# First products of the first two pairs as 256-column matmuls, under a new list of steps

## The chip, the cores and the metric

The kernel runs on one core of a Trainium2 chip. The metric is the device time of one execution in microseconds (us). The engines that matter here are TensorE (PE, with its weight loads shown as PEld), VectorE (DVE), ScalarE (ACT), GpSimd (POOL) and SyncE (SP).

## The reference

A linear attention with a decaying state feeds a two-layer network:

```python
# r, k, v: (4, 8, 768, 48); w, u: (8, 48); w_in: (384, 2048); w_out: (2048, 384)
for t in range(S):
    cur = einsum('bhd,bhe->bhde', u * k[t], v[t])
    y[t] = einsum('bhd,bhde->bhe', r[t], state + cur)
    state = w * state + einsum('bhd,bhe->bhde', k[t], v[t])
x = y.transpose(0, 2, 1, 3).reshape(B * S, H * D)      # 3072 x 384
h = x @ w_in
out = maximum(0.01 * h, h) @ w_out                     # 3072 x 384
```

## The kernel before, in words

The 3072 tokens are cut into 24 **stages** of 128 tokens, numbered 0 to 23, six to a batch. Inside a batch a stage hands its state to the next one. Two stages that follow each other form a **pair**, 0 to 11; the network works on pairs.

Nothing is scheduled at run time. One string, `ORDER` (lines 31 to 72), lists about 880 **steps** by short names, and the loop at line 801 records them in that order. Each engine then plays its own steps strictly in the listed order, and waits on semaphores only where a step reads or overwrites what a step of another engine made (`Sched`, lines 79 to 159). So the list decides two things: which step stands behind which on its engine, and what a waiting step holds up behind it. A step's name is a letter, then the stage or pair and a part, and behind `@` the PSUM bank or banks (0 to 7) that it opens. A bank can be opened again only when all readers of what was in it are done.

The letters, with the engine that plays them:

- `k`, `r`, `v` with a stage: loads of its inputs, issued by POOL; `i` with a number: a quarter of `w_in`; `w` with a number: a quarter of `w_out`, both issued by POOL. Stage 0's r and k are `p2` and `p3` and go by SP and ACT.
- `p` with a number: one-time steps. Among them `p21` (PE, spreads the row w), `p22` to `p24` (ACT, its log and two tables), `p25` and `p26` (the table of u), `p27` to `p30` (ACT, the decay over a stage, `wl`), `p16` and others (DVE, constants). `q`: DVE clears the padding of a buffer.
- `F1.512.12`: a fill; PE multiplies a matrix of ones with 512 columns (or 256, or 128) of ones, and nobody reads it (line 374).
- `P`: DVE scales r and k by the tables into `qk`. `T`, `C`: PE turns one half of `qk` (4 matmuls, line 413), ACT copies it out. From stage 8 on, `X` does the turn by a DMA transpose from SP (stages 6 and 7 and those before are turned on PE).
- `D`: DVE multiplies the turned halves (stages 0 to 5). `E`, `f`, `R`: DVE makes the diagonal's sums for the later stages. `L`: POOL spreads them into a tile.
- `A`: PE's scores (8 matmuls, line 473). `M`: DVE masks them into `at`; for some halves ACT copies (`m`) and DVE masks in place (`N`).
- `K`: PE's keys times values, for stages 0 to 5 with the diagonal's sums, for stages 1 and 2 with the carried state added (lines 527 to 536). `V`: DVE scales v by those sums. `B`, `W`: DVE makes the next state.
- `Y`: PE's outputs of a stage (lines 601 and 605). `O`: ACT copies them as `xT`.
- First product: `G` (line 634) makes four of the 16 blocks of the hidden layer for one stage, `J` (line 656) two blocks for both stages of a pair. `g` (line 644) and `j` (line 665): ACT's leaky ReLU of one such bank into `gT`.
- Second product of a pair, `w_out`: a Strassen-like scheme of seven products. `t`: DVE's sums of `w_out`'s blocks. `b`: DVE's sums of `gT`'s blocks (line 726). `Z0.0` to `Z0.6`: the seven products on PE (8 matmuls each, line 757). `z0.0` to `z0.6` (and `z11.7`): ACT or DVE takes the sums out. `o`: SP stores a stage, or half of it.

In the kernel before, pairs 0 and 1 (stages 0 to 3) go by `G`, 16 of them, and pairs 2 to 11 by `J`, 80 of them. The two differ in the columns of a matmul and in what they wait for:

```python
def up_one(n, grp):                       # G
    for f in range(4):
        for s in range(NSL):              # 3 slices of 128 of x
            PE.matmul(ps[i][:, 128 * f:128 * f + 128], w_in_sb[:, s, 128 * fb:128 * fb + 128], xT[ix][:, s, t], ...)
    add("pe", emit, R=[("xT", ix, half), ("win", grp)], W=[key])
def up_two(m, j):                         # J
    for f in range(2):
        for s in range(NSL):
            PE.matmul(ps[i][:, 256 * f:256 * f + 256], w_in_sb[:, s, 128 * fb:128 * fb + 128], xT[ix][:, s, :], ...)
    add("pe", emit, R=[("xT", ix, 0), ("xT", ix, 1), ("win", j // 2)], W=[key])
```

Of the kernel before, what the change touches and what calls it, by code (L numbers as in the profile page):

```python
# [46 lines left out]
z2.0 z0.6 J4.1@0 P15 X11 E13 J4.0@1 B9 j4.1 R10 J3.5@2 j3.4 f12 X13 L10 f13 J4.7@3 j3.5 P14 J3.7@0 j4.0 z1.5 R11
X15 Z1.6 W9 r19 b2.3 J4.4@4 o1 R12 r22 J4.5@5 X14 j4.4 j4.7 L12 A10@12 Z2.1@4 j3.7 M10 o0 k22 j4.5 K10@3 Z2.2
z1.6 B10 o3 L11 J4.6@5 R13 o2 A12@01 j4.6 L13 A11@23 M12 J4.3@7 k16 J4.2@5 M11 Z3.0@0 r16 j4.2 Z2.3@1 z2.2 W10
z2.1 b2.2 j4.3 A13@23 E15 Y10@5 f15 Y11@7 R15 Z2.4 O11 M13 O10 L15 Z2.5 z3.0 J5.6@7 k19 E14 b3.0 J5.2@5 k17 b3.1  # L50
J5.3@2 j5.2 z2.4 v13 Z3.1@3 b4.0 z2.5 J5.1@5 v14 b3.3 K12@4 Z2.6 j5.1 k23 B12 j5.3 Z3.2 z2.3 f14 k18 o4 b3.2
J5.4@5 R14 v15 A15@12 j5.4 b4.1 J5.7@4 j5.6 v20 M15 Z3.3@5 z3.2 z2.6 r17 j5.7 J5.5@7 z3.3 z3.1 K13@6 L14 Z3.4
B13 J5.0@1 z3.4 r18 b4.2 A14@45 W13 Z4.0@2 v18 M14 Z3.5 z4.0 k21 j5.5 K14@6 Z3.6 z3.5 v19 B14 Z4.1@7 P19 z3.6
j5.0 r21 W14 K15@0 P17 Y13@3 Y14@1 E18 r20 X17 b5.2 Y12@4 O14 Y15@5 f18 Z4.2 b4.3 O15 o6 O12 B15 Z4.3@1 o5 z4.1
z4.2 P18 J7.2@0 O13 E16 R18 J7.4@6 E19 z4.3 J6.5@5 E17 P16 Z4.4 j6.5 b5.0 X16 J6.6@1 f16 R16 J6.0@3 X19 b5.1 L16
J6.1@4 j6.0 E22 J6.7@5 f17 j6.1 f19 X18 z4.4 Z4.5 j7.2 R19 j6.7 J6.4@3 R17 v22 P21 o7 J6.2@0 z4.5 L17 X21 Z4.6
j6.2 L18 J7.5@7 z4.6 j7.4 J7.1@0 j6.4 L19 A16@45 j7.5 A17@23 M16 j7.1 v23 J7.7@6 Z5.0@7 k20 j7.7 M17 J6.3@0 j6.6
v21 z5.0 A19@45 j6.3 A18@12 r23 K16@6 M18 J7.6@3 Z5.1@0 j7.6 W15 K19@1 M19 J7.0@2 z5.1 Z5.2 j7.0 b6.0 Z6.0@3 B16
Z5.3@2 b5.3 z6.0 z5.2 K18@4 W16 J7.3@5 B18 Z5.4 z5.3 B19 Y16@6 b6.2 Y17@4 E21 Y18@2 E20 Y19@1 f21 z5.4 Z5.5 O19
b6.1 O18 Z6.1@1 R21 O16 P20 O17 J9.1@2 L21 j7.3 W19 X20 Z5.6 j9.1 b7.2 J8.3@6 J9.2@2 P23 z5.5 J8.0@4 X23 f22 P22  # L60
J8.2@5 f20 b7.0 Z6.2 o9 j8.2 o8 R22 J8.4@0 j9.2 X22 b6.3 j8.0 J8.7@5 R20 z6.2 j8.3 Z6.3@2 E23 L20 b7.1 j8.7
J9.0@4 z6.1 f23 j8.4 Z6.4 R23 b7.3 J9.3@0 L22 J8.5@6 z6.4 j9.3 z6.3 K20@5 Z6.5 j8.5 L23 B20 j9.0 Z6.6 z6.5 z5.6
o12 J9.6@2 z6.6 o10 J9.7@0 o11 j9.6 o13 A22@34 j9.7 A20@12 M22 A21@56 J8.6@7 J9.4@0 W20 M21 Z7.0@3 j9.4 J8.1@4
z7.0 M20 Z7.1@0 j8.1 Z7.2 j8.6 b8.0 Y21@1 Y20@2 O21 A23@45 O20 Z8.0@1 M23 J10.6@2 z8.0 b8.1 J10.3@6 K21@7 J9.5@4
B21 J10.7@5 j9.5 J10.0@7 j10.3 b9.0 z7.2 Z7.3@4 z7.1 W21 K22@6 Z7.4 B22 Z7.5 z7.4 b9.1 Z8.1@6 z7.3 Z7.6 z7.5 W22
b9.3 J10.1@4 z7.6 j10.7 b8.2 o15 Z9.0@0 j10.0 b8.3 J10.5@3 b9.2 Z8.2 j10.5 z9.0 Y22@5 j10.6 Y23@7 J10.2@3 O23
O22 J10.4@2 j10.1 J11.0@7 z8.2 j10.2 J11.3@5 z8.1 j10.4 J11.2@4 b10.0 Z8.3@3 j11.2 b10.1 Z8.4 j11.0 z8.3 j11.3
Z8.5 b10.2 Z10.0@7 z8.4 b10.3 Z9.1@2 z10.0 Z8.6 J11.5@3 z8.6 o17 J11.1@1 o14 J11.6@4 j11.1 Z9.2 j11.5 j11.6
Z10.1@5 z9.1 z9.2 J11.7@1 Z9.3@3 j11.7 J11.4@4 z10.1 Z9.4 j11.4 Z11.0@1 b11.0 Z9.5 b11.2 Z10.2 z8.5 z9.4 o16
b11.1 Z10.3@4 z10.2 z9.3 Z11.1@6 z9.5 o18 Z9.6 Z10.4 z9.6 z11.0 o19 z11.1 Z10.5 z10.4 Z11.2@0 Z11.3 z11.2 b11.3  # L70
Z10.6 z11.3 z10.5 Z11.4 z11.7 z10.6 z10.3 o23.1 Z11.5 o21 z11.4 o23.0 Z11.6@1 z11.5 o20 o22.1 z11.6 o22.0
"""


# [786 lines left out]
```

## Time and profile before

| | |
|---|---|
| median of 3 runs | 168.54 us (168.5 to 168.78) |
| the profiled execution | 168.21 us |
| its span, first to last instruction | 166.4 us |
| busy, PE / DVE / ACT / POOL | 156.9 / 129.0 / 88.5 / 89.7 us |
| matmuls on PE | 2362 |
| DMA | 19.69 MB in 100092 packets |

The span is what the trace shows; 1.8 us of the execution lie around it. Busy time of PE counts a matmul from its start to its modelled end, so overlapping ones are not counted twice, and a matmul that waits inside the pipeline counts as busy. Idle time of an engine costs only where another waits for it.

### The profile page before, as it was taken

What the parts mean: (1) busy time and instruction counts of PE and PEld (TensorE: products, weight loads), DVE (VectorE), ACT (ScalarE), POOL (GpSimd) and SP (SyncE); (2) the same over time, 40 slices, a digit from 0 to 9 for tenths busy, and PEclk for the clock granted to TensorE, in tenths of its full rate; (3) what the DMA queues carried; (4) which work ended last, traced back from release to release, by engine and by line L of the source; (5) the groups of instructions that cost most, each with busy time, mean ns of one, the idle gap of its engine ahead of it and who ended that gap; (6) DMA issues with size and microseconds to landing.
All of it is one profiled execution on the core that took longest, in us unless ns stands there. A gap on an engine that the chain in (4) does not pass through costs nothing.

```text
span 166.4 us, 5494 instructions
## 1 busy us (share of the span) xinstructions
PE 156.9 (94%) x2362; PEld 138.9 (83%) x2362; DVE 129.0 (78%) x261; ACT 88.5 (53%) x195; POOL 89.7 (54%) x101
## 2 busy tenths in 40 slices
...
GB/s 98 117 117 143 146 191 168 162 204 183 141 137 143 119 134 154 192 213 69 149 98 128 195 138 154 67 4 98 190 149 44 0 4 47 6 2 96 47 96 189
DMA packets 100092, 19.69 MB, mean 118 GB/s; under 512 B 93154, under 2 KB 100068, under 8 KB 100068
## 3 DMA queue, kind: packets, MB, share of 16 engines
...
q1 hardware_dynamic: 22514, 9.12, 26.8%
...
## 4 chain that ended last, share of the span: by engine, by line
PE 77%; DVE 11%; issue 3%; DMA 3%; ACT 2%; POOL 2%; DVEq 0%; POOLq 0%
PE ps_all L757 30%; PE ps_all L656 28%; PE ps_all L601 5%; PE ps_all L634 4%; PE ps_all L473 4%; DMA rk_sb<-in_r_dram 3%; DVE gs L726 2%; PE ps_all L413 2%; POOL rk_sb L274 2%; PE ps_all L531 2%; DVE ku L434 2%; DVE s_tok L444 1%; DVE at L497 1%; DVE qk L391 1%; ACT tp L424 1%
## 5 line engine op out<-in xcount | busy, mean ns | idle before, releaser
L665 ACT ACTIVATE gT<-ps_all 128x512 bf16<-128x512 f32 x80 | 44.8, 604 | 31.9 <-PE ps_all L656 28.6
L656 PE MATMUL ps_all<-xT,w_in_sb 128*128 128x256 bf16 x480 | 58.9, 273 | 0.1
L656 PEld LDWEIGHTS ps_all<-xT,w_in_sb 128*128 128x128 bf16 x480 | 45.5, 98 | 5.7 <-DVE out_sb L778 0.3
L459 POOL TENSOR_SCALAR_AFFINE_SELECT at<-s_tok 128x1024 bf16<-128x1024 f32 x18 | 22.3, 1254 | 31.7 <-DVE s_tok L444 31.7
L726 DVE TENSOR_TENSOR gs<-gT 128x1024 bf16<-128x1024 bf16 x24 | 17.8, 745 | 15.6 <-ACT gT L665 8.4
L757 PE MATMUL ps_all<-tw,gs 128*128 128x192 bf16 x288 | 28.9, 246 | 0.0
L497 DVE CAST_PREDICATED at<-mask,ps_all 128x1024 bf16<-128x1024 uint16 x18 | 21.7, 1219 | 6.6 <-PE ps_all L473 6.2
L757 PEld LDWEIGHTS ps_all<-tw,gs 128*128 128x128 bf16 x288 | 24.0, 98 | 0.7
L274 POOL DMA_DIRECT2D v_sb<-in_v_dram x24 | 22.6, 960 | 0.0
L274 POOL DMA_DIRECT2D rk_sb<-in_r_dram x23 | 21.8, 956 | 0.3 <-issue 0.3
L274 POOL DMA_DIRECT2D rk_sb<-in_k_dram x23 | 21.3, 937 | 0.0
L757 PE MATMUL ps_all<-w_out_sb,gT 128*128 128x192 bf16 x192 | 19.5, 246 | 0.0
L768 ACT ACTIVATE snap<-ps_all 128x192 f32<-128x192 f32 x36 | 11.3, 341 | 11.9 <-PE ps_all L757 11.8
L757 PEld LDWEIGHTS ps_all<-w_out_sb,gT 128*128 128x128 bf16 x192 | 16.1, 98 | 0.6
L619 ACT ACTIVATE xT<-ps_all 128x384 bf16<-128x384 f32 x24 | 11.0, 494 | 10.5 <-PE ps_all L601 8.7
L778 DVE TENSOR_TENSOR out_sb<-ps_all,snap 128x192 f32<-128x192 f32 x37 | 12.4, 351 | 2.9 <-PE ps_all L757 2.7
L391 DVE TENSOR_TENSOR qk<-rk_sb,tab 128x768 bf16<-128x768 bf16 x23 | 12.6, 550 | 2.2 <-DMA rk_sb<-in_r_dram 1.2
L634 PE MATMUL ps_all<-xT,w_in_sb 128*128 128x128 bf16 x192 | 12.4, 219 | 0.4 <-issue 0.2
L634 PEld LDWEIGHTS ps_all<-xT,w_in_sb 128*128 128x128 bf16 x192 | 11.0, 98 | 1.0 <-issue 0.4
L601 PE MATMUL ps_all<-at,v_sb 128*32 128x128 bf16 x384 | 10.7, 220 | 0.9 <-issue 0.9
L644 ACT ACTIVATE gT<-ps_all 128x512 bf16<-128x512 f32 x16 | 8.8, 603 | 4.6 <-PE ps_all L634 4.6
L424 ACT ACTIVATE tp<-ps_all 128x512 bf16<-128x512 f32 x16 | 8.8, 596 | 4.4 <-PE ps_all L413 4.3
...
## 6 DMA issues: line engine op xcount, KB each, us to landing
...
tp<-qk SPq DMA_TRANSPOSE x16, 4.2
```

Of the source, the lines that this page charges most:

```text
L274: add("pool", lambda: G.dma_start(dst, src), W=[key], dma=f"{which}{n}")
L391: add("dve", lambda: V.tensor_tensor(qk[iq][:, :, 0:D], both, by, ALU.mult), R=[("r", n % NRK), ("k", n % NRK), "qtab", "ktab", ("qk0", iq ...
L459: add("pool", lambda: G.affine_select(out=at[ia][:, :, :, :].rearrange("p two m i -> p (two m) i"), in_=s_tok[i2][:, :].unsqueeze(2).to_br ...
L497: add("dve", lambda: V.copy_predicated(dst, mask[:, :].bitcast(mybir.dt.uint16).unsqueeze(1).to_broadcast([128, H, 128]), raw), R=keys + [ ...
L601: last = PE.matmul(ps_y[32 * q:32 * q + 32, 128 * s:128 * s + 128], a, m, start=first_mm and (s == 0 or whole), stop=last_mm and whole)
L634: last = PE.matmul(ps[i][:, 128 * f:128 * f + 128], w_in_sb[:, s, 128 * fb:128 * fb + 128], xT[ix][:, s, t], start=s == 0, stop=s == NSL - 1)
L656: last = PE.matmul(ps[i][:, 256 * f:256 * f + 256], w_in_sb[:, s, 128 * fb:128 * fb + 128], xT[ix][:, s, :], start=s == 0, stop=s == NSL - 1)
L665: add("act", lambda: A.activation(gT[ig][:, 2 * j:2 * j + 2, :].rearrange("p f t -> p (f t)"), ps[i][:, :], AF.Prelu, alpha=0.01), R=[key] ...
L726: add(eng, lambda: on.tensor_tensor(x[i][:, :, :], a, b, op), R=keys, W=[("gs", m % 2, i)])
L757: done = PE.matmul(ps[i][:, 0:NH], lhs[:, s, :], rhs[:, s, :], start=bool(opens) and s == 0, stop=s == HF - 1, skip_group_check=not (opens ...
L768: add("act", lambda: A.activation(snap[i2][j][:, :], ps[i][:, 0:NH], AF.Copy), R=[key], W=[("snap", i2, j)])
L778: add("dve", lambda: V.tensor_tensor(out_sb[io][:, cols], ps[i][:, 0:NH], snap[i2][j][:, :], ALU.add), R=[key, ("snap", i2, j), *after], W ...
```

## The change

Two things are edited, both in `ORDER`; no function changes. Pairs 0 and 1 now go by `J` and `j` as the others do: 16 `G` and 16 `g` leave the list, `J0.0` to `J0.7`, `J1.0` to `J1.7` and their `j` come in. And the whole list is in another order, with other PSUM banks, and with 23 fills in place of 11 (7,296 columns in place of 3,840). All other steps are the same set. The start, up to the first second product, of the old list and the new:

```diff
-p1 p0 p9 p19 q4 p18 p2 r2 q1 p3 q3 p15 p4 p11 p8 q2 p10 p5 p21@0 k2 q0 p14 p13 p12 p17 p6 p16 k1 p7 F1.512.12@1
-p22 r1 p20 p23 k5 p24 P0.0 r5 P0.1 T0.0@7 q5 F1.512.6@6 p31 v0 C0.0 F1.256.8@5 P2 T0.1@6 r3 p25@7 C0.1 T2.1@0 k3
-T2.0@1 P1 C2.1 D0 T1.1@2 v1 p32 T1.0@0 C1.1 P5 F1.512.1@3 i1 C1.0 F1.256.11@4 A0@23 C2.0 v2 D1 A1@45 M0.1 p27
-p28 A2@01 k6 F1.512.3@6 T5.1@3 F1.256.7@6 C5.1 P3 F1.256.9@6 r6 T5.0@6 m1.1 M0.0 T3.1@3 p29 k4 M2 K0@5 p30
-T3.0@2 C3.1 v3 C5.0 F1.256.4@3 B0 F1.256.13@0 C3.0 V0 r4 K1@3 D2 A3@56 B1 r7 F1.256.3@0 Y0@1 M3.0 K2@2 k7 M1.0
-O0 p26 A5@01 N1.1 i0 G0.1@5 D3 V2 i3 P6 g0.1 Y2@4 v4 V1 T6.0@7 M5.0 O2 T6.1@5 r9 Y1@3 C6.0 D5 B2 C6.1 K3@4 k9
-G2.1@0 P4 O1 m5.1 M3.1 T4.0@7 r8 T4.1@5 C4.0 V3 G1.1@2 P7 C4.1 i2 Y3@3 N5.1 g1.1 v7 E7 T7.1@1 B3 O3 A4@56 D4 v5
-T7.0@7 f7 C7.0 E6 G2.0@2 v6 f6 C7.1 R6 G0.0@7 g2.1 k8 M4 G3.1@1 L6 G1.0@0 g3.1 W3 G3.0@3 g0.0 w2 K4@1 g3.0 w3
-G3.3@4 B4 g1.0 V4 G0.3@3 g3.3 E9 G1.3@5 R7 g2.0 f9 g0.3 L7 A7@67 b0.2 A6@01 g1.3 Y4@4 M6 K5@5 G3.2@2 w0 W4
-G1.2@3 R9 g3.2 w1 V5 G0.2@0 g1.2 L9 M7 G2.3@5 r11 K6@1 b1.0 K7@2 g2.3 Y5@3 O4 B6 v8 G2.2@7 b0.0 O5 k11 Y6@1 b0.1
-Y7@6 k10 E8 J2.5@5 O7 B7 g2.2 J2.3@6 P9 k13 g0.2 b1.2 X9 J2.4@7 O6 k12 W7 j2.3 J2.1@0 f8 P8 r13 J2.0@6 R8 X8
-b0.3 J2.2@4 v9 b1.1 J2.7@3 j2.2 r14 J2.6@2 v12 t0 J3.0@1 j2.6 J3.1@4 j2.1 r10 t1 j2.4 Z0.0@2 k15 J3.3@0 j3.1 r12
+p1 p0 p9 q0 p11 p2 p19 r1 p10 p3 p4 q1 p8 F1.256.2@0 p12 p16 p5 p21@7 k1 p6 p20 k2 p7 p14 p15 F1.512.14@6 p13
+F1.256.15@5 p22 r2 F1.256.13@6 p25@0 p23 F1.256.9@1 F1.128.2@2 k5 F1.512.15@3 p24 P0.0 F1.512.13@4 p26 P0.1 k3
+F1.512.19@5 T0.0@6 r3 F1.256.0@7 F1.512.12@0 C0.0 P1 T0.1@7 p28 r5 p18 q5 F1.512.6@0 q2 p17 C0.1 q3 T1.1@1 v0 P2
+A0@23 p31 C1.1 D0 v1 T1.0@0 p32 M0.1 F1.256.16@1 T2.1@4 C1.0 i1 M0.0 T2.0@1 C2.1 P3 v2 F1.128.5@0 F1.512.4@5
+C2.0 D1 T3.0@0 q4 F1.256.17@7 F1.256.6@6 P5 p30 v3 A1@12 C3.0 A2@34 p27 F1.256.11@5 M2 F1.128.7@7 k4 F1.128.6@6
+T5.1@0 p29 T5.0@5 C5.1 K0@7 T3.1@6 r4 m1.1 B0 F1.256.8@0 C5.0 M1.0 K1@0 k6 C3.1 F1.128.3@4 V0 F1.512.8@5 r6 B1
+A3@12 A5@34 N1.1 Y0@5 D2 i0 V1 k7 D3 K2@6 M3.1 Y1@7 r7 V2 K3@0 M3.0 O1 Y2@2 v4 O0 V3 J0.2@7 B2 O2 i3 P4 Y3@1 v5
+M5.0 T4.1@2 P6 O3 T4.0@5 i2 J0.3@6 C4.1 E6 k9 f6 m5.1 J1.3@3 B3 C4.0 J1.2@4 w0 j0.2 D4 A4@01 D5 j0.3 r9 T6.1@2
+J0.1@5 C6.1 v6 T6.0@7 j1.3 J0.0@6 P7 j0.1 w1 J1.1@2 R6 j1.2 M4 C6.0 K4@3 L6 T7.1@5 j1.1 J1.0@4 w2 W3 C7.1 T7.0@7
+B4 K5@0 J1.7@1 w3 V4 J1.6@2 N5.1 r8 j1.7 E7 V5 J0.6@5 C7.0 v7 f7 j0.0 W4 Y4@3 j1.6 b0.2 k8 A6@01 O4 A7@67 j0.6
+E9 Y5@2 R7 J1.4@3 M6 L7 O5 J0.5@5 J0.7@2 j0.5 J0.4@0 f9 j1.0 R9 j0.7 J1.5@1 M7 j0.4 L9 J2.4@2 j1.4 J2.5@0 v8
+b0.0 j1.5 P9 J2.7@7 r13 b1.2 X9 J2.0@1 b1.0 k12 J2.6@6 j2.0 b0.1 J2.1@5 k11 j2.5 b1.1 J2.3@1 j2.1 v9 b0.3 K6@0
+j2.4 J2.2@4 B6 k13 j2.6 Z0.0@5 t0 r14 Z1.0@0 b1.3 r10 Y6@6 t2 z1.0 Y7@3 O6 Z0.1@2 r12 O7 j2.3 K7@6 J3.3@3 v12 E8
...
+Z0.6 E13 j3.0 z0.3 r15 b2.1 Z1.4 j3.4 r16 z0.6 A8@67 z1.4 J3.5@3 M8 r17 K9@1 Z1.5 k22 P12 Y9@5 B9 Y8@6 P14 Z1.6
+O8 E10 P10 O9 J3.7@1 z1.6 f11 X10 P13 J4.6@0 j3.7 P11 J4.4@7 R11 X12 f13 J4.5@1 j4.4 W9 f10 J4.0@6 j3.5 f12 X11
+b2.2 j4.6 J4.7@5 R12 J4.1@7 R10 L12 o1 R13 J4.3@3 X13 j4.1 z0.5 Z2.0@0 L10 j4.7 j4.5 K10@7 J4.2@2 X14 L13 j4.3
+B10 Z3.0@5 z1.5 j4.0 P15 L11 z2.0 A10@34 j4.2 A12@67 X15 M10 z3.0 J3.6@1 v13 Z2.1@2 j3.6 o2 M12 v14 Z2.2 o0
...
```

More of the change, by code (lines that the diff above doesn't have):

```diff
@@ L42 @@
-Y7@6 k10 E8 J2.5@5 O7 B7 g2.2 J2.3@6 P9 k13 g0.2 b1.2 X9 J2.4@7 O6 k12 W7 j2.3 J2.1@0 f8 P8 r13 J2.0@6 R8 X8
-b0.3 J2.2@4 v9 b1.1 J2.7@3 j2.2 r14 J2.6@2 v12 t0 J3.0@1 j2.6 J3.1@4 j2.1 r10 t1 j2.4 Z0.0@2 k15 J3.3@0 j3.1 r12
-Z1.0@7 j3.0 j2.5 Z0.1@4 v10 P11 j2.0 J3.2@1 b1.3 z0.0 v17 j3.3 Z1.1@5 t3 j3.2 r15 Z0.2 j2.7 E11 t2 z1.0 v11
-Z0.3@6 z0.2 z1.1 z0.1 K8@3 b2.0 k14 A9@01 Z0.4 z0.3 M9 L8 Z1.2 Z0.5 v16 B8 z1.2 z0.4 A8@01 W8 Z1.3@6 b2.1 J3.6@3
-M8 Z0.6 E10 Z1.4 P13 j3.6 z0.5 Y8@0 P10 Y9@1 O8 z1.3 X10 Z1.5 z1.4 O9 P12 Z2.0@6 E12 f11 X12 f10 K9@3 J3.4@4
@@ L47 @@
[L47 to L71, printed above, removed]
+p1 p0 p9 q0 p11 p2 p19 r1 p10 p3 p4 q1 p8 F1.256.2@0 p12 p16 p5 p21@7 k1 p6 p20 k2 p7 p14 p15 F1.512.14@6 p13
@@ new lines @@
+b0.0 j1.5 P9 J2.7@7 r13 b1.2 X9 J2.0@1 b1.0 k12 J2.6@6 j2.0 b0.1 J2.1@5 k11 j2.5 b1.1 J2.3@1 j2.1 v9 b0.3 K6@0
+j2.4 J2.2@4 B6 k13 j2.6 Z0.0@5 t0 r14 Z1.0@0 b1.3 r10 Y6@6 t2 z1.0 Y7@3 O6 Z0.1@2 r12 O7 j2.3 K7@6 J3.3@3 v12 E8
+j2.2 P8 J3.2@1 j3.3 B7 X8 v10 Z1.1@4 t1 z0.0 j2.7 k14 J3.1@6 j3.2 W7 t3 Z1.2 k10 Z0.2 b2.0 z1.2 r11 j3.1 Z0.3@3
+f8 z0.1 R8 z0.2 k15 K8@1 z1.1 A9@67 B8 Z0.4 L8 M9 Z0.5 r19 J3.4@1 E11 z0.4 W8 k16 Z1.3@6 J3.0@7 v11 z1.3 E12
+Z0.6 E13 j3.0 z0.3 r15 b2.1 Z1.4 j3.4 r16 z0.6 A8@67 z1.4 J3.5@3 M8 r17 K9@1 Z1.5 k22 P12 Y9@5 B9 Y8@6 P14 Z1.6
@@ new lines @@
+O8 E10 P10 O9 J3.7@1 z1.6 f11 X10 P13 J4.6@0 j3.7 P11 J4.4@7 R11 X12 f13 J4.5@1 j4.4 W9 f10 J4.0@6 j3.5 f12 X11
+b2.2 j4.6 J4.7@5 R12 J4.1@7 R10 L12 o1 R13 J4.3@3 X13 j4.1 z0.5 Z2.0@0 L10 j4.7 j4.5 K10@7 J4.2@2 X14 L13 j4.3
+B10 Z3.0@5 z1.5 j4.0 P15 L11 z2.0 A10@34 j4.2 A12@67 X15 M10 z3.0 J3.6@1 v13 Z2.1@2 j3.6 o2 M12 v14 Z2.2 o0
+Z2.3@1 b2.3 k19 z2.2 z2.1 A11@34 W10 A13@67 v16 M11 Z2.4 k18 Z2.5 z2.4 E15 Y10@3 v22 b3.0 Y11@4 O10 M13 Z2.6 r22
+O11 K12@3 J5.5@4 z2.6 r20 f15 E14 J5.1@0 B12 j5.5 E16 J5.6@6 z2.5 j5.1 R15 J5.3@7 z2.3 L15 b3.1 A15@01 j5.3
```

21 lines of the change are left out of this document (added).

## The prediction

> **What bounds the kernel now.** I read the page's busy shares, then the windows of 5 us, then the chain that ended last, then the timeline where that chain leaves the matmuls.
>
> ```profile
> PE 156.9 (94%) x2362; PEld 138.9 (83%) x2362; DVE 129.0 (78%) x261; ACT 88.5 (53%) x195; POOL 89.7 (54%) x101
> ```
> ```profile
> 0.00:5.00 5.00, 2.18 (x3) 0.59 (x3) 3.58 (x15) 2.29 (x4) 4.03 (x9) 1.00 0.84 99
> 5.00:10.00 5.00, 3.57 (x24) 2.44 (x25) 2.86 (x8) 2.81 (x6) 5.00 (x7) 1.00 2.71 123
> 10.00:15.00 5.00, 5.00 (x55) 3.54 (x54) 3.87 (x6) 3.26 (x8) 5.00 (x7) 1.00 1.58 125
> 15.00:20.00 5.00, 3.97 (x79) 2.71 (x76) 4.39 (x10) 2.85 (x7) 5.00 (x7) 1.00 2.59 145
> 20.00:25.00 5.00, 5.00 (x147) 4.45 (x145) 5.00 (x12) 4.54 (x10) 5.00 (x7) 1.00 1.54 185
> 25.00:30.00 5.00, 4.98 (x93) 4.62 (x91) 3.83 (x9) 3.73 (x8) 4.87 (x6) 1.00 2.14 168
> 30.00:35.00 5.00, 4.76 (x112) 4.32 (x110) 5.00 (x9) 3.19 (x7) 2.63 (x3) 1.00 1.96 176
> 35.00:40.00 5.00, 3.94 (x116) 3.26 (x113) 4.97 (x10) 1.92 (x4) 4.82 (x6) 1.00 1.33 202
> ```
> (Columns: stretch, its length, then busy time and count of PE, weight loads, DVE, ACT, POOL; granted clock, DMA.) PE looks busy everywhere, but a pipelined matmul counts as busy while it waits, so I measure PE by its rates in the chain:
>
> ```profile
> 4.18 4.61 DMA rk_sb<-in_r_dram
> ...
> 9.50 1.03 PE ps_all L413 x8
> ...
> 20.84 0.45 PE ps_all L413 x8
> 21.29 0.51 PE ps_all L601 x28
> 21.79 0.27 PE ps_all L605 x3
> 22.07 0.08 PE ps_all L527 x4
> 22.14 0.19 PE ps_all L531 x4
> ...
> 23.49 0.67 PE ps_all L634 x12
> ...
> 35.62 0.84 PE ps_all L634 x12
> ...
> 38.92 0.91 issue
> ...
> 40.12 6.66 PE ps_all L656 x60
> ...
> 52.22 0.33 PE ps_all L473 x8
> ...
> 57.71 0.90 PE ps_all L601 x56
> ...
> 74.62 1.97 PE ps_all L656 x18
> ...
> 97.97 0.28 DVE out_sb L778
> 98.30 1.48 PE ps_all L656 x12
> ...
> 153.70 9.91 PE ps_all L757 x120
> 163.64 0.36 DVE out_sb L778
> ```
> Full rates of the steps: half a turn T 0.223 us (0.45/2); scores A 0.33; G 0.67; J 0.655 (1.97/3); Z 0.66 (9.91/15); keys-values K 0.27 with its sums, 0.17 without, 0.16 more where a state is carried; outputs Y 0.62 (28 of 16 ns, by 0.90 for 56, and 3 of 56 ns), 0.43 for Y0; the two row products 0.76. **Arrears** of a PE step are its start less all PE work listed ahead of it, fills left out. Ahead of J2.5, the first product of pair 2 (40.06, where the run of 60 begins), the old list has 16 T 3.57, 8 A 2.64, 16 G 10.69, K0 to K7 2.11, Y0 to Y7 4.24 and 0.76: 24.0. Arrears 16.05. The whole list is 146.17, and PE ends at 153.70 + 9.91 = 163.61: arrears 17.44. So after 40 us PE loses 1.4 us in 123; the time is decided ahead of it.
>
> What sets arrears there is DVE: 3.58, 2.86, 3.87, 4.39, 5.00, 3.83 and 5.00 are 28.5 us of work in 35 us, so it has waited 6.46.
>
> ```profile
> 7.51 0.56 DVE L391 TENSOR_TENSOR qk<-rk_sb,tab 128x768 bf16<-128x768 bf16 x1 [0.66 <-DMA rk_sb<-in_k_dram]
> ...
> 8.88 0.56 DVE L391 TENSOR_TENSOR qk<-rk_sb,tab 128x768 bf16<-128x768 bf16 x1 [0.81 <-DMA rk_sb<-in_r_dram]
> ...
> 15.46 0.56 DVE L562 TENSOR_TENSOR st<-ps_all,wl 128x384 bf16<-128x384 f32 x1 [0.81 <-ACT wl L325]
> ...
> 21.72 0.55 DVE L562 TENSOR_TENSOR st<-ps_all,wl 128x384 bf16<-128x384 f32 x1
> ...
> 30.67 0.35 DVE L434 TENSOR_TENSOR ku<-rk_sb,u_tab 128x384 bf16<-128x384 bf16 x1
> ...
> 31.67 1.57 DVE L726 TENSOR_TENSOR gs<-gT 128x1024 bf16<-128x1024 bf16 x1
> ...
> 35.03 0.54 DVE L552 TENSOR_TENSOR vs<-v_sb,ps_all 128x384 bf16<-128x384 bf16 x1
> ```
> The rule I use: a PE step that waits for a DVE step has arrears of at least (DVE work through that step) − (PE work ahead of the waiter) + (what DVE has waited). Test: G2.3 at 35.62 reuses the bank that V5 (35.03) reads. DVE work through V5 is 29.03, PE work ahead of G2.3 21.00: 8.03 + 6.46 = 14.49; the trace has 35.62 − 21.00 = 14.62. The handover is 0.13. Behind it the old list has Y5, Y6 and Y7 and the pause of 0.91 at 38.92, which no semaphore explains, and so comes to 16.05.
>
> **The change part by part.** *The wide products.*
>
> ```profile
> L656 PE MATMUL ps_all<-xT,w_in_sb 128*128 128x256 bf16 x480 | 58.9, 273 | 0.1
> ...
> L665 ACT ACTIVATE gT<-ps_all 128x512 bf16<-128x512 f32 x80 | 44.8, 604 | 31.9 <-PE ps_all L656 28.6 <-PE ps_all L757 3.1
> ...
> L634 PE MATMUL ps_all<-xT,w_in_sb 128*128 128x128 bf16 x192 | 12.4, 219 | 0.4 <-issue 0.2
> L634 PEld LDWEIGHTS ps_all<-xT,w_in_sb 128*128 128x128 bf16 x192 | 11.0, 98 | 1.0 <-issue 0.4 <-DVE vs L552 0.3 <-ACT tp L424 0.2
> ...
> L644 ACT ACTIVATE gT<-ps_all 128x512 bf16<-128x512 f32 x16 | 8.8, 603 | 4.6 <-PE ps_all L634 4.6
> ```
> 192 matmuls of 128 columns go (16 × 0.67 = 10.69), 96 of 256 come (16 × 0.655 = 10.48): PE gains 0.21. ACT pays 603 or 604 ns for the same 16 gates: nothing. A matmul pair is 56 ns in the row (0.67/12) and 109 (1.97/18). The Trainium skill ("TensorE: Matmul & The Clock Gate", Back-to-back issue gap) states for a sustained stream some 81 ns at 128 columns and 131 at 512; by it the change would save between 3 us (192 × 81 − 96 × 131) and 7.8 (96 × 81 left). The rows disagree with that and agree with the page's isolated gap of N/2.4 + 2.5 ns; the sum goes by the rows.
>
> *What is late next.* J0.2 needs both stages' x, G0.1 needed one; Y3 and the turns T4 are queued behind it on PE. It needs ACT's O0, listed behind O1, which reads Y1. From Y1's end to J0.2, ACT has 0.13 less to do than PE, so Y2 and K3 hide it; uncovered it costs one copy, 0.5.
>
> *DVE's order.* Ahead of V5 the new list has 4.62 us less: the eight steps E9, R7, f9, b0.2, M6, W4, R9 (all that DVE did from 30.67 to 35.03, 4.36) and f7 (0.27) come behind V5. Through V5 it is 24.41. Through B2 (old list 16.90 at 22.19, where the next step starts) P6, M5.0 and D5 go (1.40) and M3.1, V3 come (1.06): 16.56.
>
> *DVE's wait.* r1 and k1 are now POOL's first two loads, in the place of r2 and k2. The second load released DVE at 7.51, and P1 now stands there, behind 3.58 of work: wait 3.93. Old: 2.68 there, 5.29 by 22 us, among it 0.81 for r1 at 8.88 and 0.81 for wl at 15.46. In the new list the two exponentials for wl stand on ACT ahead of C5 and m1.1. r5 becomes POOL's eighth load; the fourth went out at 4.18 and landed 4.61 later, so at 0.87 us a load r5 lands near 12.3, and DVE comes to P5, behind 8.54 of work, at 12.5. I take 4.05, with a tenth for handovers; bounds 3.93 and 5.29.
>
> *Arrears, new.* Ahead of Y3, which waits for B2's state: 10 T, 5 A, K0 to K3, Y0 to Y2, one J, 0.76 = 8.37. So 16.56 − 8.37 + 4.05 + 0.13 = 12.4. The next demands are lower: V5 to Y5 24.41 − 18.86 = 5.55; M6 to J0.4 28.30 − 21.44 = 6.86, where the old list had its 8.03. So PE no longer waits for DVE up to J2.4, which now stands ahead of K6, K7, Y6 and Y7. I add 0.9 for changes between kinds of steps (the row's 0.78 for a Y against 0.62, the like at A and T) and half the pause of 0.91: arrears 13.8, J2.4 at 22.75 + 13.8 = 36.5.
>
> *Fills.* 3,456 columns more. Nine fills F stand ahead of T0.0. PE is slow at first (8 turns in 1.03 at 9.50, against 0.45 at 20.84; some 1 ns a column), and at that rate they put T0.0 at about 6.8, a microsecond behind its operand. With one turn, two fills, the copy C0.1 and the scores behind it, A0 ends near 9.8. DVE comes to M0.1, the first step that needs A0, at 6.29 + 3.93 = 10.2: hidden by 0.4; uncovered, a fill more costs its own length, up to 0.5.
>
> *POOL and SP.* The last block of w_out moves up from POOL's 37th place to its 33rd, some 4 us earlier; the old list's Z0.0 ran after 30.56 us of PE's work, the new one's is due at 28.16 + 13.8 = 42, 4.6 us earlier, which about balances. v7 falls back from 28th to 35th, some 6 us; K7 and Y7, its readers, fall back by over 6 us of PE's work. If w_out lands late, t0 and then Z1.2 wait for it; the slack there is about 1 us. On SP o1 passes X13 and X15, but what it stores is done before P13 is. None of these ends last.
>
> *After 40 us.* PE keeps its 1.4 of losses. New are loops PE to DVE to PE with hardly any slack. From the end of A8, M8 to z0.5 is 9.40 on DVE, while PE reaches J4.2, which needs z0.5's bank, in 9.12: 0.28 lost. Two more: M18 to z6.3 and J8.3, 15.13 against 14.95: 0.18; M11 to z2.3 and A15, −0.07. The old list's tightest, z3.4 to z4.5 and J7.5 (97.97, 98.30), came to −0.03 and cost about 0.3. I take 0.7 in all; bounds 0 and 1.4.
>
> **Sum.** PE's end: 146.17 − 0.21 + 13.8 + 1.4 + 0.7 = 161.86, against 163.61: 1.75 us. The tail behind the last product stays. The profiled execution took 168.21, so 166.5; the median of the runs is 168.54, so **166.8**.
>
> **The rivals.**
> - *More is won.* No pause and no loop: another 1.15, 165.6. For it: in the first loop f13 is priced with its own row, in which two such steps take 1.51 us,
>
> ```profile
> 61.91 1.51 DVE L439 TENSOR_TENSOR ku<-rk_sb,ku 128x384 bf16<-128x384 bf16 x2
> ```
> where the usual one takes 0.27 to the next. Against: these loops are the tightest in the list.
> - *The narrow stream pays for its weights.* If the 98 ns weight loads (11.0 us for 192) paced the 128-column products, halving them would win about 5 us more: 162. Against it stands 0.67 for 12. This is what the page's stream rule would mean here.
> - *PE is what is late ahead of 12 us*, and the fills bring its fast rate sooner: that gives nothing while DVE sets the start, so it has no number of its own. The Trainium skill (same page, What's actually happening) states that the array's clock doubles after one busy window of about 3.4 us; the rows have the change after 9.50 and before 20.84, and no row here shows what fills do to it.
> - *DVE's wait stays at 5.29*, if a load or ACT is as late as now: 1.24 back, 168.0.
> - *Slower: DVE takes PE's place in the middle.* DVE is in order, so a loop that ends late holds up the next. If each of the six tightest (0.28, 0.18, −0.07, −0.19, −0.30, −0.32) costs 0.6 of handover in place of the 0.3 at 98.30, they take 3.2 instead of 0.7: 169.3. It decides from 0.55 a loop. For it: the chain runs over DVE up to 97.97. Against: it cost PE 0.3 there in all.
> - *The change does not do what it says*: only the wider matmul counts, and the order's demands merely move: 0.2, 168.3.
>
> **How the numbers follow.** Main forecast 0.48 (166.8; 165.8 to 167.8 by the bounds of wait, pause and loops), more won 0.15, weights 0.02, wait stays 0.10, nothing 0.08, slower 0.17. A difference of 0.2%, 0.34 us, is what a measurement can tell. Faster 0.75, same 0.08, slower 0.17. The range 165.3 to 168.9 leaves out most of the slower case and the end of the best one.
>
> **What would show it.** Right: P1 at 7.5; V5 at 28.5 to 30; J2.4 at 36 to 37; the last Z product ends near 162. Wrong: DVE idle over 5 us before 20 us; a gap on PE of 0.5 or more at J4.2, A15 or J8.3; or J2.4 behind 38.

## The result, and the profile after

| | before | changed |
|---|---|---|
| first comparison, median of all six executions | 168.84 us | 170.53 us (166.18 to 171.65) |
| the two executions that enter the ratio | | 166.18, 166.5 us |
| ratio changed to before | | 0.985 [0.982, 0.989], about 166.3 us |
| second comparison (E1), median of 29 and 12 | 168.28 us | 166.72 us (165.94 to 170.6) |
| ratio there | | 0.992 [0.988, 0.995], about 166.9 us |

The forecast was 166.8 us. The ratios leave out executions more than 1.5% above the fastest of their kernel: four of the first six (169.93 to 171.65 us, among them the profiled one of 171.6) and three of the twelve in E1. What these lose, and why, is the subject of the first experiments; the median of all 18 is 167.3 us. Line numbers of the changed kernel are higher by two than before (L413 is now L415, L778 is L780).

An execution of 166.09 us (from E1), first the chain that ended last, then DVE's instructions in order of time:

```profile
32.14 7.86 PE ps_all L658 x72
...
152.61 7.28 PE ps_all L759 x88
```
```profile
7.51 0.56 DVE L393 TENSOR_TENSOR qk<-rk_sb,tab 128x768 bf16<-128x768 bf16 x1 [1.22 <-DMA rk_sb<-in_k_dram]
...
19.89 0.55 DVE L564 TENSOR_TENSOR st<-ps_all,wl 128x384 bf16<-128x384 f32 x1
...
28.52 0.55 DVE L554 TENSOR_TENSOR vs<-v_sb,ps_all 128x384 bf16<-128x384 bf16 x1
```
P1 stands at 7.51, B2 at 19.89 (before 21.72) and V5 at 28.52 (before 35.03). The run of 72 matmuls is twelve J products, and J2.4 is the sixth: 32.14 + 5 × 0.655 = 35.4. With 22.75 of PE's work ahead of it, its arrears are 12.7, where the old list had 16.05. The run of 88 ends at 159.89, and two more products of 0.66 bring PE's end to 161.2, against 163.61.

Now the execution of 171.6 us: its chain, then DVE, PE and SP's queue in order of time, and PE's stretches with the granted clock.

```profile
32.73 7.86 PE ps_all L658 x72
...
70.11 7.10 DMA out_dram<-out_sb
...
157.88 7.28 PE ps_all L759 x88
```
```profile
77.24 0.36 DVE L780 TENSOR_TENSOR out_sb<-ps_all,snap 128x192 f32<-128x192 f32 x1 [2.91 <-DMA out_dram<-out_sb]
```
```profile
78.38 0.79 PE L475 MATMUL ps_all<-tp 48*128 48x128 bf16 x16 [2.82 <-DVE out_sb L780]
```
```profile
63.55 1.74 SPq L693 DMA_DIRECT2D out_dram<-out_sb  x1
65.34 4.11 SPq L404 DMA_TRANSPOSE tp<-qk  x3
69.50 1.50 SPq L693 DMA_DIRECT2D out_dram<-out_sb  x2
```
```profile
75.00:80.00 5.00, 2.18 (x58) 1.68 (x59) 2.76 (x5) 1.31 (x3) 1.80 (x2) 0.87 1.64 101
80.00:85.00 5.00, 5.00 (x61) 4.27 (x49) 4.96 (x9) 2.63 (x7) 2.67 (x4) 0.79 1.21 144
```
The start is 0.6 us later than in the other execution (32.73 against 32.14). The time goes in the middle. SP issues the transposes X13, X14 and X15, then o2 and o0, and o0, issued at 70.11, lands at 77.2. There are four output buffers, and stage 4 uses that of stage 0 again: DVE's z2.5 stands 2.91 us until o0 has landed, z2.3 stands behind it, and A15 needs the bank that z2.3 reads, so PE stands 2.82 us, from 75.56 to 78.38. The granted clock falls only when PE is at work again: by stretches of 1 us it is 1.00 up to 78, then 0.84, three times 0.50, 0.95, and 1.00 again from 83 on. (The two lines above have the means of 5 us, 0.87 and 0.79.) From J2.4 to PE's end 7.3 us are lost here (157.88 + 7.28 + 1.32 − 145.96 = 20.5 of arrears, against 32.73 + 3.28 − 22.75 = 13.3), 2.6 in the execution of 166.09 us.

### The profile page after: what moved, and what is told of

It reads as the page before. It is cut to its first block, busy times and chain, and to the rows that moved or that the text cites. A ratio compares the mean times of both kernels' runs of the same rounds, so it can differ in the third digit from the quotient of the medians.

```text
span 169.9 us, 5318 instructions
## 1 busy us (share of the span) xinstructions
PE 159.0 (94%) x2278; PEld 138.4 (81%) x2278; DVE 129.3 (76%) x261; ACT 88.8 (52%) x195; POOL 88.2 (52%) x101
## 4 chain that ended last, share of the span: by engine, by line
PE 69%; DMA 12%; POOL 10%; DVE 4%; issue 2%; SPq 1%; DVEq 0%; POOLq 0%
PE ps_all L658 31%; PE ps_all L759 28%; POOL rk_sb L276 7%; DMA out_dram<-out_sb 7%; DMA w_in_sb<-in_moe_w_in_dram 5%; PE ps_all L603 5%; PE ps_all L475 3%; POOL v_sb L276 3%; PE ps_all L533 1%; DVE at L499 1%; DVE out_sb L780 1%; POOL w_in_sb L282 1%; DVE s_tok L446 1%; DVE gs L728 0%; SPq L693 0%
## 5 line engine op out<-in xcount | busy, mean ns | idle before, releaser
L658 PE MATMUL ps_all<-xT,w_in_sb 128*128 128x256 bf16 x576 | 71.3, 274 | 1.1 <-DVE out_sb L780 0.9
L658 PEld LDWEIGHTS ps_all<-xT,w_in_sb 128*128 128x128 bf16 x576 | 54.7, 98 | 8.0 <-DVE out_sb L780 1.2
L461 POOL TENSOR_SCALAR_AFFINE_SELECT at<-s_tok 128x1024 bf16<-128x1024 f32 x18 | 20.6, 1161 | 40.5 <-DVE s_tok L446 31.3
L728 DVE TENSOR_TENSOR gs<-gT 128x1024 bf16<-128x1024 bf16 x24 | 16.2, 684 | 10.3 <-ACT gT L667 10.3
L780 DVE TENSOR_TENSOR out_sb<-ps_all,snap 128x192 f32<-128x192 f32 x37 | 12.5, 352 | 13.8 <-DMA out_dram<-out_sb 6.3
L393 DVE TENSOR_TENSOR qk<-rk_sb,tab 128x768 bf16<-128x768 bf16 x23 | 13.9, 611 | 2.0 <-DMA rk_sb<-in_k_dram 1.4
L475 PE MATMUL ps_all<-tp 48*128 48x128 bf16 x192 | 8.4, 224 | 3.3 <-DVE out_sb L780 2.8
L426 ACT ACTIVATE tp<-ps_all 128x512 bf16<-128x512 f32 x16 | 9.3, 606 | 2.6 <-PE ps_all L415 2.4
L475 PEld LDWEIGHTS ps_all<-tp 48*128 48x128 bf16 x192 | 5.7, 96 | 6.0 <-DVE out_sb L780 3.1
L603 PEld LDWEIGHTS ps_all<-at,v_sb 128*32 128x32 bf16 x384 | 8.5, 100 | 2.2 <-issue 1.2
```

The lines of the kernel that those rows point to most:

```text
L393: add("dve", lambda: V.tensor_tensor(qk[iq][:, :, 0:D], both, by, ALU.mult), R=[("r", n % NRK), ("k", n % NRK), "qtab", "ktab", ("qk0", iq ...
L461: add("pool", lambda: G.affine_select(out=at[ia][:, :, :, :].rearrange("p two m i -> p (two m) i"), in_=s_tok[i2][:, :].unsqueeze(2).to_br ...
L475: last = PE.matmul(ps[i][:, 128 * p:128 * p + 128], tp[it][at_rows, NP + p, :], tp[it][at_rows, p, :], start=True, stop=True)
L603: last = PE.matmul(ps_y[32 * q:32 * q + 32, 128 * s:128 * s + 128], a, m, start=first_mm and (s == 0 or whole), stop=last_mm and whole)
L658: last = PE.matmul(ps[i][:, 256 * f:256 * f + 256], w_in_sb[:, s, 128 * fb:128 * fb + 128], xT[ix][:, s, :], start=s == 0, stop=s == NSL - 1)
L728: add(eng, lambda: on.tensor_tensor(x[i][:, :, :], a, b, op), R=keys, W=[("gs", m % 2, i)])
```

## The experiments

Two questions: what makes executions of 170 us, and which part of the edit moved the start of pair 2.

**E1, the changed kernel once more.**

> The changed kernel once more, unedited, to see how far its executions differ. The forecast's theory: product J2.4 starts near 35.8 to 36.5 us in every execution, and the time is 166.2 to 166.8 us whenever no wait stands in the middle. The store theory (DVE's z2.3 overwrites an output buffer whose store o0 is issued by SP behind DMA transposes and lands late; PE then idles 2.8 us ahead of A15 and its clock falls): the executions split in two groups, near 166.3 us and near 170 to 171.6 us, and a profile of the first group shows no wait of DVE's z2.3 for the store over 0.5 us, at the same start of J2.4. A rival, that the start itself is unsteady: J2.4 would differ between such executions by 2 us or more.

166.72 us, twelve executions; three of them took 169.84, 170.42 and 170.6 us, the others 165.94 to 168.22. DVE's waits for stores in the profiled one:

```profile
73.56 0.36 DVE L780 TENSOR_TENSOR out_sb<-ps_all,snap 128x192 f32<-128x192 f32 x1 [0.47 <-DMA out_dram<-out_sb]
...
112.71 0.62 DVE L780 TENSOR_TENSOR out_sb<-ps_all,snap 128x192 f32<-128x192 f32 x2 [1.02 <-DMA out_dram<-out_sb]
...
150.91 0.36 DVE L780 TENSOR_TENSOR out_sb<-ps_all,snap 128x192 f32<-128x192 f32 x1 [1.87 <-DMA out_dram<-out_sb]
```
The same places wait in the better execution too, 0.47 us instead of 2.91 at the first: z2.5 for o0, z5.3 for o6, and z9.3 for o14. The groups are less sharp than the store theory had it (167.86 and 168.22 lie between them). The start differs little: 32.14 and 32.73 for the run of 72. That puts J2.4 at 35.4 in the better execution, 0.4 ahead of what was expected. The three executions near 170 us have no profile of their own; that they lose their time as the one of 171.6 us did is argued from E2.

**E2, six output buffers.**

```diff
-RINGS = (6, 6, 6, 6, 6, 3, 3, 4, 14)
+RINGS = (6, 6, 3, 6, 6, 3, 3, 6, 14)
```

> Output buffers six in place of four (three in place of six for the buffers of the scaled v make the room). Then z2.3 overwrites a buffer that no earlier store reads, and z6.3 waits for o6 in place of o8, issued over ten us earlier. The store theory: no wait of DVE for a store in the middle, no idle of PE over 0.7 us at A15, and every execution near 166.0 to 166.8 us. The rival, that PE's clock drops by itself and the wait only shows it: executions near 170 to 171.6 us go on as often as without the edit. The price of three buffers for the scaled v: 0 to 0.5 us.

165.72 us (165.48 to 166.42), ratio to before 0.988 [0.984, 0.991]. The waits of DVE for `out_sb` and the stretch that held the idle time:

```profile
DVE out_sb L780 <- PE ps_all L759: 7.5, 7, 1.8
...
DVE out_sb L780 <- ACT snap L770: 1.0, 1, 1.0
...
DVE out_sb L780 <- issue: 0.4, 1, 0.4
```
```profile
75.00:80.00 5.00, 5.00 (x101) 4.59 (x96) 4.01 (x9) 3.87 (x9) 4.68 (x4) 1.00 1.19 98
```
No store is among the releasers any more, PE is not idle in that stretch, and its clock stays at 1.00. A repeat (E12) gave 165.15 to 166.09. None of 12 executions with six buffers came near 170 us, and 7 of 18 with four did. So the clock falls because PE stood, and not the other way round: without the stop there is no fall, and in the execution of 171.6 us the fall comes behind the stop.

**E3, narrow products in the new list.**

```diff
-... J0.2@7 B2 O2 i3 P4 Y3@1 v5 ...
+... G0.1@7 B2 O2 i3 P4 Y3@1 v5 ...
```
and so on for all 16 products of pairs 0 and 1 and their gates.

> The new list with the 16 wide products of pairs 0 and 1 put back as 16 narrow ones (128 columns, one stage each) in the same places and banks. The forecast's rows: 16 x 0.67 in place of 16 x 0.655, so 0.2 us more than the changed kernel, with J2.4 0.2 later. The rival that narrow products are paced by their weight loads: 3 to 7.8 us more than the changed kernel. If the wide form were all that the change does, this kernel would be back near 168.3 to 168.8 us.

168.26 us (167.24 to 169.4), 1.5 more than E1 and level with before (1.002 [0.999, 1.005]). That would fit the wide form as the only gain, but the trace holds another reason:

```profile
152.52 0.62 DVE L780 TENSOR_TENSOR out_sb<-ps_all,snap 128x192 f32<-128x192 f32 x2 [3.92 <-DMA out_dram<-out_sb]
```
Here the store wait at the third place is 3.92 us, against 1.87 in E1. The run could not tell the two apart; E6 does.

**E4, the stores moved ahead, four buffers.**

```diff
-... j4.1 z0.5 Z2.0@0 ... X14 ... X15 ... o2 M12 v14 Z2.2 o0 ...
+... j4.1 z0.5 o0 Z2.0@0 ... X14 ... X15 ... o2 M12 v14 Z2.2 ...
```
and o8 right behind z4.5.

> The changed kernel with two stores moved ahead on SP: o0 from behind the transposes X14, X15 and store o2 to right behind z0.5, which it stores, and o8 ahead of o9. No buffer is added. The store theory: z2.3 finds its buffer free, the 2.8 us of idle ahead of A15 goes, and all executions come near 166.0 to 166.8 us; if only the ring's size mattered and not the place of the store on SP's queue, executions of 170 to 171.6 us would go on. The price: X14 and X15 are issued up to 1 us later, hidden, since E14 and what follows on DVE read them some 9 us later.

167.08 us (165.98 to 171.08). The wait for o0 is gone, the two others stay:

```profile
112.78 0.62 DVE L780 TENSOR_TENSOR out_sb<-ps_all,snap 128x192 f32<-128x192 f32 x2 [1.29 <-DMA out_dram<-out_sb]
...
150.96 0.36 DVE L780 TENSOR_TENSOR out_sb<-ps_all,snap 128x192 f32<-128x192 f32 x1 [1.85 <-DMA out_dram<-out_sb]
```
One execution of twelve still took 171.08 us; it has no profile. In the profiled one the place on SP's queue decides for o0. But o8, which I had taken for the second one, is not waited for: z5.3 waits for o6 and z9.3 for o14, both of which the new list issues late. So the expectation was wrong in the store that it named, and the ring of four is too short for this list in three places.

**E5, six buffers in the kernel before.**

> The kernel before with six output buffers in place of four (and three for the scaled v in place of six). Its trace shows no wait of DVE for a store. Theory that the ring matters only under the new list: no more than 0.3 us off the kernel before. Rival, that six buffers are worth their 0.7 us or more in any list: 0.7 us or more faster, and then the changed kernel with six buffers would have to be compared with this one.

168.58 us, ratio 1.000 [0.997, 1.003]. (One of the twelve executions took 869.55 us, which nothing on record explains; the others 167.32 to 168.91.) The ring costs nothing in the old list, so the store wait was brought in by the new one. The profiled execution, of 167.32 us, shows something else:

```profile
35.12 0.47 DVE vs L552
...
39.00 6.67 PE ps_all L656 x60
```
Up to V5 it agrees with the profile of the kernel before (there the chain has V5 at 35.11), but the pause of 0.91 at 38.92 is not there, pair 2 begins 1.1 us earlier (39.00 against 40.12), and the execution is 0.89 shorter. So this pause, which no semaphore explains, is in some executions of the old list and not in others. The experiments that follow have six buffers, unless they say otherwise, so that the store wait does not blur them.

**E6, E3 with six buffers.**

> The new list with narrow products for pairs 0 and 1, and six output buffers, so that no store wait stands in the comparison with the changed kernel with six buffers (165.7 us). By the rows, 16 x 0.67 against 16 x 0.655: 0.2 us more, 165.9 us. If the wide form is worth more than its rows show (its weights, its instructions, its use of the clock): 166.7 us or more, and PE's first product of pair 2 would start 0.8 us later or more.

166.25 us (165.97 to 166.77), against 165.72 in E2 and 165.55 in E12: 0.5 to 0.7 more. By ratios to before it is 0.987 [0.984, 0.989] against 0.988 and 0.983, which does not separate them. The groups of the page, and the chain:

```profile
L636 PE MATMUL ps_all<-xT,w_in_sb 128*128 128x128 bf16 x192 | 11.9, 219 | 0.0
...
L636 PEld LDWEIGHTS ps_all<-xT,w_in_sb 128*128 128x128 bf16 x192 | 11.0, 98 | 0.4 <-issue 0.4
```
```profile
32.54 3.35 PE ps_all L636 x60
35.89 4.58 PE ps_all L658 x42
```
Five narrow products take 3.35, that is 0.67 each, in a run in which nothing else stands in the way, and pair 2 begins at 35.9. E2 has 32.62 + 3.28 = 35.9, with a pause of PE of 0.34 ahead of it that nothing explains; E12, without a pause, has 32.37 + 3.28 = 35.65. The weight loads of 98 ns pace nothing: a narrow matmul takes 56 ns here (3.35/60). That leaves 0.2 by the rows, and up to 0.5 that no row shows and that the ratios can't tell from nothing.

**E7, no fills.** All 23 `F` are taken out of the new list.

> The changed kernel with six output buffers and without its 23 fills, whose sums nobody reads. The forecast's theory: DVE sets the start, the fills lie in PE's waits, so J2.4 moves by less than 0.3 us and the time stays at 165.7 within 0.3 us. The rival that the fills bring PE's fast rate sooner and that this is what moved the start: the turns stay at 0.5 us of PE each beyond 12 us, Y3 comes 1 to 3 us later, and the time is 166.7 to 168.7 us.

167.53 us (167.14 to 168.24), 1.8 more than E2; the ratio to before is 0.994 [0.992, 0.997], clear of E2's and E12's. The run of 72 comes 1.3 us later than in E2 (32.62) and 1.6 later than in E12 (32.37):

```profile
33.96 7.86 PE ps_all L658 x72
```
**E9, fewer fills:**

```diff
-F1.256.2@0  F1.256.15@5  F1.256.13@6  F1.256.9@1  F1.128.2@2  F1.512.15@3  F1.512.13@4
-F1.512.19@5  F1.256.0@7  F1.512.12@0          (all ahead of A0)
```

> The changed kernel with six output buffers and 13 of its 23 fills: ten ahead of A0 are taken out, so that 3,840 columns are left, as many as the kernel before has. The forecast's theory (the added fills are hidden and bring nothing): J2.4 within 0.2 us of 35.95, the time within 0.3 us of 165.7. The rival (the fills bring PE's fast rate sooner, and without any of them J2.4 came 1.1 us later): the fast rate comes at 13 us or later in place of 10.3, M2 on DVE waits longer for A2, J2.4 comes 0.5 to 1.1 us later, the time is 166.3 to 167.5 us.

166.86 us: four of six executions took 166.86 to 166.96, two 165.48 and 165.86. E12, in the same set of runs with all fills, has 165.55. PE's turns, all of them in one line (smallest, median and largest duration in ns), in the kernel before, in E9 and in E12:

```profile
L413 PE MATMUL ps_all<-ident,qk x60: 217/314/314, 6.2 to 24.9; 128*128 128x128 bf16 x60
```
```profile
L415 PE MATMUL ps_all<-ident,qk x48: 219/314/314, 5.9 to 23.2; 128*128 128x128 bf16 x48
```
```profile
L415 PE MATMUL ps_all<-ident,qk x52: 219/219/314, 7.0 to 24.4; 128*128 128x128 bf16 x52
```
A turn's matmul lasts 314 ns while PE is slow and 219 when it is fast. With the fills most turns are fast ones; without them, as before the change, most are slow. (E9 has as many columns of fills as the old list in all, but only 1,024 of them ahead of A0, where the old list has 2,048 and the new one 4,480.) DVE's instructions in order of time in E9, and then in E12, with the chain of each, show what that does:

```profile
13.96 1.23 DVE L496 TENSOR_TENSOR at<-ps_all,mask 128x1024 bf16<-128x1024 f32 x1 [1.21 <-PE ps_all L475]
15.85 0.56 DVE L564 TENSOR_TENSOR st<-ps_all,wl 128x384 bf16<-128x384 f32 x1 [0.66 <-PE ps_all L533]
...
21.50 0.55 DVE L564 TENSOR_TENSOR st<-ps_all,wl 128x384 bf16<-128x384 f32 x1
```
```profile
33.76 7.86 PE ps_all L658 x72
```
```profile
13.12 1.22 DVE L496 TENSOR_TENSOR at<-ps_all,mask 128x1024 bf16<-128x1024 f32 x1 [0.38 <-PE ps_all L475]
14.26 0.55 DVE L564 TENSOR_TENSOR st<-ps_all,wl 128x384 bf16<-128x384 f32 x1
...
19.84 0.55 DVE L564 TENSOR_TENSOR st<-ps_all,wl 128x384 bf16<-128x384 f32 x1
```
```profile
32.37 7.86 PE ps_all L658 x72
...
151.84 7.27 PE ps_all L759 x88
```
DVE waits 1.21 for the slow scores A2 in place of 0.38, and 0.66 for K0 in place of nothing; B2 comes at 21.50 in place of 19.84, and the run of 72 at 33.76 in place of 32.37. So in the profiled executions the ten fills are worth 1.4 us at the start and 1.2 in the time (166.87 against 165.64), where the forecast had nothing. Over all six executions the size is less sure: by the ratios, 0.989 [0.984, 0.993] against 0.983 [0.979, 0.987], it is 0.9 us, and the intervals overlap. Why two executions without them were as quick as with them is open; no profile of one was taken.

**E10, the same added fills alone, in the kernel before (four buffers).**

```diff
-p7 F1.512.12@1 p22 ... T0.0@7 q5 F1.512.6@6
+p7 F1.512.12@1 F1.256.2@2 F1.256.15@3 F1.256.13@4 F1.256.19@2 F1.128.2@3 F1.512.15@4
+F1.512.13@2 F1.512.19@3 p22 ... T0.0@7 F1.256.0@4 F1.512.20@2 q5 F1.512.6@6
```

> The kernel before with ten more fills ahead of T0.0 and T0.1, the same 3,456 columns that the new list has more; nothing else is changed. The forecast's theory: DVE's waits for loads and for the decay table set the head, so the time stays within 0.3 us. The rival that the fills alone make the gain: fast rate near 10.5 us in place of 14.65, the first product of pair 2 a microsecond or more earlier, the time 1 to 2 us below the kernel before.

167.25 us against 168.63, ratio 0.993 [0.991, 0.995]: 1.2 us less with the fills, in the old order. The turns, B2 on DVE, and the chain:

```profile
L413 PE MATMUL ps_all<-ident,qk x60: 219/219/314, 6.7 to 24.5; 128*128 128x128 bf16 x60
```
```profile
21.25 0.55 DVE L562 TENSOR_TENSOR st<-ps_all,wl 128x384 bf16<-128x384 f32 x1
```
```profile
27.10 0.46 issue
...
35.31 0.47 DVE vs L552
...
39.19 6.67 PE ps_all L656 x60
```
B2 comes 0.47 earlier than before (21.72), but that is lost again by V5 (35.31 against 35.11 in the chains), in a pause of PE of 0.46 at 27.10 that nothing in the profile explains. Pair 2 begins 0.93 earlier than before (40.12) because the pause of 0.91 at 38.92 is missing, and it is missing in E5 too, which has no added fills and begins pair 2 at 39.00. So the time is shorter with the fills, but this profile does not show them shortening a wait of DVE's that lasts up to pair 2. How they bring all twelve executions below 168 us is open.

**E8, more work for DVE ahead of B2.** `P5` stands three times in a row in place of once.

> The changed kernel with six output buffers, and the DVE step P5 played three times in a row in place of once (it writes the same values again): two times 0.56 to 0.61 us more of DVE's work ahead of B2, behind the last load that DVE waits for. The rule of the forecast (arrears of PE = DVE work through the step less PE work ahead of the waiter, plus DVE's waits): Y3 and J2.4 start 1.1 to 1.2 us later, and the end moves by as much, to 166.8 us. The rival, that PE, ACT or the loads set the head and DVE has slack there: J2.4 moves by less than 0.4 us.

166.29 us, 0.6 to 0.7 more than E2 and E12. DVE and the chain:

```profile
12.21 1.68 DVE L393 TENSOR_TENSOR qk<-rk_sb,tab 128x768 bf16<-128x768 bf16 x3
13.81 1.22 DVE L496 TENSOR_TENSOR at<-ps_all,mask 128x1024 bf16<-128x1024 f32 x1
...
20.61 0.55 DVE L564 TENSOR_TENSOR st<-ps_all,wl 128x384 bf16<-128x384 f32 x1
```
```profile
32.97 7.86 PE ps_all L658 x72
```
Of the 1.2 us added, 0.38 goes into the wait for A2, which is gone; B2 comes 0.77 later and the run of 72 comes 0.6 later than in E12 (0.35 than in E2). By the ratio, 0.987 [0.985, 0.990], the time is not told apart from E2's 0.988 [0.984, 0.991]. So the rule's 1.1 to 1.2 us were too much; whether the rival's bound of 0.4 holds depends on the run that it is compared with, and E2's profile has the pause of 0.34 us. What the waits show is that in the head DVE and PE set the pace in turn, and what DVE is late, it in part gives back where it would have waited for PE.

**E11, V5 behind five of the moved steps again.**

```diff
-... E7 V5 J0.6@5 ... j0.0 W4 Y4@3 j1.6 b0.2 k8 A6@01 ... E9 Y5@2 R7 ... f9 j1.0 R9 ...
+... E7 J0.6@5 ... j0.0 b0.2 E9 R7 f9 R9 V5 W4 Y4@3 j1.6 k8 A6@01 ... Y5@2 ... j1.0 ...
```

> The changed kernel with six output buffers, with V5 and W4 of DVE moved back behind five of the steps that the new list had put behind them (b0.2, E9, R7, f9, R9). The rule gives DVE's work through V5 27.63 less PE's work ahead of A6, whose bank V5 reads, 18.20: 9.43 in place of 6.21, plus DVE's wait of 3.9 and 0.13, arrears 13.5 at A6 where the trace has 12.9 to 13.1; so J2.4 0.4 to 0.7 us later and the time 166.1 to 166.4 us. If DVE's order there were nothing that PE waits for: J2.4 within 0.1 us.

171.66 us (171.09 to 172.5), 6.1 more than E12. DVE, PE and the stretch behind it:

```profile
30.53 0.69 DVE L728 TENSOR_TENSOR gs<-gT 128x1024 bf16<-128x1024 bf16 x1 [0.91 <-ACT gT L667]
...
33.08 0.36 DVE L441 TENSOR_TENSOR ku<-rk_sb,ku 128x384 bf16<-128x384 bf16 x1 [1.12 <-DMA rk_sb<-in_r_dram]
...
33.94 0.54 DVE L554 TENSOR_TENSOR vs<-v_sb,ps_all 128x384 bf16<-128x384 bf16 x1
```
```profile
34.63 0.62 PE L475 MATMUL ps_all<-tp 48*128 48x128 bf16 x16 [3.65 <-DVE vs L554]
```
```profile
35.00:40.00 5.00, 4.71 (x61) 3.50 (x56) 2.66 (x3) 1.30 (x3) 5.00 (x7) 0.66 1.85 177
```
V5 comes at 33.94 and PE stands 3.65 us for it. V5's place decides, as the forecast had it, but the price was far off: the rule counted DVE's work and took its waits as given, and ahead of V5 there now stand a wait of 0.91 for a gate and one of 1.12 for the load of r9, at steps that the new list has behind it. After the stop the granted clock is 0.66 over five microseconds.

**E12** is E2 again, on the same chip as E9 to E11.

> The changed kernel with six output buffers once more, on the same chip as the three others: 165.5 to 166.4 us, without any execution near 170 us. Were the first six only lucky, one in three would come out at 169.8 us or more.

165.55 us (165.15 to 166.09), ratio 0.983 [0.979, 0.987]. With six buffers each of the twelve executions (165.15 to 166.42 us) is shorter than the shortest of the kernel before in these comparisons (167.03), and both medians lie below that of the changed kernel with four (166.72 in E1).

## Why the prediction was right or wrong

The time was right by both ratios (166.8; 166.3 and 166.9), and so were the marks it gave for P1 (7.51) and V5 (28.52). In part that was luck: errors of opposite sign met, and 7 of 18 executions took 3.5 to 5.5 us longer than the rest, the profiled one because of a wait that the forecast did not have. Two steps failed: the fills and the stores.

- **The wide products** (0.21 us): held. Five narrow products take 3.35 us (E6). The rival in which the weights pace them would have made about 5 us; E6 shows 0.2 to 0.7. By an estimate from the stream figures of the Trainium skill ("TensorE: Matmul & The Clock Gate", Back-to-back issue gap) it would have been 3 us or more, which E6 does not bear out.
- **DVE's order**: held in kind. With the old number of fill columns, the new list still wins 1.8 us (E9, 166.86 against 168.63; the wide products are in that), and V5 put back costs PE 3.65 us (E11). The rule's sizes hold only while DVE's waits stay where they are (E8, E11).
- **DVE's wait, 4.05 in place of 5.29**: the size was right, the reason was half of it. B2 starts behind 16.56 − 0.55 = 16.01 us of DVE's work; in E12 at 19.84, so DVE has waited 3.83. The forecast put that down to r1 and k1 being loaded first and to the order on ACT. Those waits do go: the old list's 0.81 and 0.39 for loads of r and 0.81 for wl are 0.18 in all in E12, and none in E9. But without the ten fills waits for PE stand in their place, 1.21 for A2 and 0.66 for K0, and with B2 at 21.50 E9 has 5.49 of waiting.
- **Fills hidden, "that gives nothing while DVE sets the start"**: this is the step that failed at the start. In the new list DVE's wait is in part a wait for PE at its slow rate, so a faster PE shortens it: by 1.49 for A2 and K0 (E9 against E12). Taking away the ten fills gives back 0.9 us by the ratios and 1.3 by the medians, near what the forecast had priced, at 1.24, as the rival in which the wait stays; taking away all 23 gives back more (E7). So the 4.05 came out through a term that the forecast had put at nothing. In the old list the fills win 1.2 us as well (E10), but its profile does not show them winning it in this way.
- **Arrears at J2.4, 13.8**: 12.7. The 0.9 for changes between kinds of steps and half the pause of 0.91 were too much: Y3 had been foreseen at 12.4, and not much is added behind it.
- **POOL and SP, "none of these ends last"**: this is the step that failed behind the start. The forecast looked at o1 and not at o0, whose buffer z2.5 writes again, nor at o6 and o14. In the old list no DVE step waits for a store; in the new one o0 lands just in time or late.
- **Later loops, 0.7, with 1.4 of losses kept, 2.1 in all**: 2.6 with four buffers and 1.6 with six (151.84 + 7.27 + 1.32 − 145.96 = 14.5, less 32.37 + 3.28 − 22.75 = 12.9). The loop ahead of A15 was named, and the gap stands there (2.82 us where 0.5 was the mark for wrong), but it waits for a store and not for DVE's work. The slower rival, 169.3, had that place and not that mechanism; 7 of 18 executions took its time or more.
- **The tail stays**: it grew by 0.3. PE ends 2.4 us earlier (161.2 against 163.61), while the execution is 2.1 shorter (166.09 against 168.21).

So errors of opposite sign hid behind a good number: in the execution of 166.09 us the start was 1.1 us better than foreseen, and what follows 0.8 worse (0.5 in the later loops, 0.3 in the tail). The profile that the forecast started from also holds the pause of 0.91 us that other executions of the kernel before lack (E5).
